# Top-k attention and a gated MLP on one core: the weight preparation spread over twelve slots for ten, and four steps of the opening moved

## The chip, the core and the metric

The kernel runs on one core of a Trainium2 chip. The metric is device time in microseconds (us); lower is better. Five engines work in it, each through its own queue in order: TensorE (PE: matmuls, and PEld, the loading of their weights), VectorE (DVE), ScalarE (ACT), GpSimd (POOL), and SyncE (SP), which issues the DMAs. An engine waits only at the head of its queue, so one late operand holds everything that is queued behind it.

## The reference

Attention over 8 batches, 8 heads, 576 rows and a head dimension of 64, in which each row keeps its 32 largest scores, and then an MLP with a gate. Everything is float32.

```python
scores = scale * np.matmul(q, k.transpose(0, 1, 3, 2))
kth = np.partition(scores, -top_k, axis=-1)[..., -top_k:-top_k + 1]
scores = np.where(scores >= kth, scores, -1e9)
attn = np.exp(scores - np.max(scores, axis=-1, keepdims=True))
attn = attn / (np.sum(attn, axis=-1, keepdims=True) + 1e-09)
x = np.matmul(attn, v)                # to (4608, 512): heads side by side
h = x @ w_in                          # 512 to 2048
out = (h / (1 + np.exp(-1.702 * h))) @ w_out
```

## The kernel before

**Slots.** The attention is cut into 144 slots, 18 for each batch. A slot is 128 rows of two heads (or the 64 last rows of four). For a slot n the steps are, by function:

- `scores`: PE makes the 128x576 scores of two heads in PSUM (`s_ps`); ACT copies them to SBUF (`sc`, line 238).
- `topk`: DVE finds the 32 largest of each row by fourteen passes, eight of MAX8 (line 247) and six of MATCH_REPLACE8 (line 250).
- `bounds`: POOL makes two small tiles, `cut` and `low`, from the 32nd and the first value (lines 266 and 267).
- `exponentials`: ACT makes the masked exponentials `pr` (lines 275 and 277) and their sums `den`.
- `divide`: DVE makes 1/`den` (lines 286 and 288, tiles `some` and `rden`). For n below SETTLED, POOL then writes `by`, a diagonal of the reciprocals, two of 128x128 (line 292), of which there is one buffer; later, ACT and POOL scale one head of `pr` each (lines 294 and 295).
- `turn_main`, `turn_ends`: PE turns `pr` (line 308 by a matmul with `by`, line 306 by a plain transpose), and ACT copies the result to `pt` (line 316).
- `values`: PE multiplies with v (line 338), ACT copies to `xT` (line 350).

When the four head pairs of a row block are done, `hidden` (PE, line 381, four groups for one row block), `tanh` (ACT, line 398), `gate` (DVE, line 414, or with `aside` POOL, lines 411 and 412, which needs a copy `h` by ACT, line 401) and `project` (PE, line 429) do the MLP for it. `gT` has four buffers, so at most four gated groups wait for `project`.

**Weights.** A float32 weight is not used as it was loaded: `round_piece` remakes each of 32 pieces of 128x512 in steps on three engines: "size" (ACT, line 144), "shift" (DVE, line 145), "low" (ACT, line 147), "sign" (ACT, line 146), and "finish" (POOL, lines 140 and 141, two operations). The text calls "finish" a weight step. The pieces of slot n are loaded in slot n-1 and their finishes run in slot n+1; `raws` has eight buffers for the loads. The first 16 pieces are `win`, the others `wout`.

**The order.** It is written out by hand. `opening` prepares the first two head pairs. Then `slot(n)` runs for n = 0 to 9 (SETTLED = 9): the "single slots", which interleave topk(n) with the exponentials, the turning and the values of n-1, the scores of n+2, and the weight pieces of `by_slot[n]`. From slot 10 on, `two_slots(n)` handles two slots at a time: a "pair". Single slots use the DVE gate; pairs use POOL's. `project` starts in slot 8 (PROJECTS = 7). Inside topk, the queues are filled at set places:

```python
if i == 2 and unfinished:
    unfinished.pop(0)()           # one weight step
if i == 5:
    if before: divide(n - 1)
    while unfinished: unfinished.pop(0)()
```

In a pair, all weight steps left over go into topk at one a place, ahead of the POOL work of `divide` and of `gate`, and ahead of `bounds` of the next slot. `stay_warm` adds matmuls whose results nobody uses.

Of the kernel before, what the change touches and what calls it, by code (L numbers as in the profile page):

```python
# [28 lines left out]
def kernel(  # L29
# [37 lines left out]
    CC = C // P  # L67
    FC = DFF // P
    G = 4
# [7 lines left out]


    PROJECTS = 7
    SETTLED = 9  # L80
    assert D == 64 and 2 * TAIL == P and C == NP * P and C == PIECE and B % 2 == 0
    assert TOPK == 32 and NP == 4 and NF == 4 and NG == 4 and CC == 4

# [74 lines left out]
    def stay_warm(count, of=ident[:]):  # L158

        none = ps_p.tile([P, C], F32, name="none", tag="po")  # L160
        for i in range(count):
            nc.tensor.matmul(none[:, 0:P], lhsT=of, rhs=of, start=True, stop=True)
# [58 lines left out]
    def scores(n):  # L221
        b, t, hps = slots[n]
        ps = [ps_s.tile([P, 2, 512], F32, name="s_ps") for _ in range(2)]
        if t < NF:
            parts = [(i, 0, slice(0, P), slice(t * P, (t + 1) * P)) for i in range(2)]
        else:
            parts = [(i, p, slice(p * TAIL, (p + 1) * TAIL), slice(FULL, S)) for i, p in ((0, 0), (1, 1), (0, 1), (1, 0))]
        for c in range(2):
            for i, p, rows, cols in parts:
                on = slice(i * D, (i + 1) * D)  # L230
                nc.tensor.matmul(  # L231
                    ps[i][rows, c, 0:HALF],
                    lhsT=qT[b, hps[p]][on, cols],
                    rhs=kT[b, hps[p]][on, FIRST[i] + c * HALF : FIRST[i] + (c + 1) * HALF],
                )
        sc = st[n]["sc"] = scp.tile([P, 2, S], F32, name="sc")
        for i in range(2):
            nc.scalar.copy(out=sc[:, i, :].rearrange("p (c k) -> p c k", c=2), in_=ps[i][:, :, 0:HALF])  # L238
# [30 lines left out]
    def exponentials(n):  # L269

        sc, cut, low = st[n]["sc"], st[n]["cut"], st[n]["low"]
        pr = st[n]["pr"] = prp.tile([P, 2 * S], F32, name="pr")
        den = st[n]["den"] = small.tile([P, 2], F32, name="den")
        for i in range(2):
            nc.scalar.activation(sc[:, i, :], sc[:, i, :], AF.Prelu, bias=cut[:, i : i + 1], alpha=HUGE)  # L275
        for i in range(2):
            nc.scalar.activation(  # L277
                pr[:, i * S : (i + 1) * S], sc[:, i, :], AF.Exp, bias=low[:, i : i + 1],
                accum_out=den[:, i : i + 1],
            )  # L280
# [37 lines left out]
    def turn_main(n):  # L318
        for i in range(2):
            turn(n, i * NF, MAIN[i], NF)  # L320

    def turn_ends(n):

        turn(n, 2 * NF, FULL, 1)
# [122 lines left out]
    READY = (((-9, -8), (-7, -6), (-4, -3), (-2, -1)), ((-7, -6), (-4, -3), (-3, -2), (-1, -2)))  # L447
    FETCH = (((-13, -12), (-11, -10), (-7, -7), (-5, -4)), ((-11, -10), (-9, -8), (-5, -5), (-2, -2)))
    VALUES = ((-8, -7, 0, 0), (-8, -7, 2, 2))
    by_slot = dict(enumerate([2, 2, 3, 3, 3, 3, 4, 4, 4, 4]))  # L450
    for n in by_slot:
        first = sum(map(len, list(by_slot.values())[:n]))
        by_slot[n] = list(range(first, first + by_slot[n]))
# [9 lines left out]
    for b in range(1, B):  # L463
        for hp in range(NP):
# [2 lines left out]
                at(b * PER + READY[b % 2][hp][i], prepare, name, b, hp)  # L467
            at(b * PER + VALUES[b % 2][hp], load_v, b, hp)
    unfinished = []

    early = []

    def opening():

        stay_warm(7, v_ends[0][:].rearrange("p j d -> p (j d)"))
        for hp in range(2):
            for name in "qk":
                load(name, 0, hp)
        for x in by_slot[0]:
            load_piece(x)  # L480
        for m in range(2):
            for name in "qk":
                prepare(name, 0, m)
            if m == 1:
                early.extend(round_piece(x) for x in by_slot[0])
                for piece in early:
                    piece["size"]()
            scores(m)
        for hp in range(2, NP):
            for name in "qk":  # L490
                load(name, 0, hp)
        load_v(0, 0)
        for x in by_slot[1]:
            load_piece(x)

    def slot(n):
        todo = later.pop(n, [])
        for fn, args in todo:
            if fn is not prepare:
                fn(*args)  # L500
        preparing = [args for fn, args in todo if fn is prepare]
        settled = n > PROJECTS
        aside = SETTLED < n < N
        before = 0 <= n - 1 < N
        if before:
            bounds(n - 1)
            exponentials(n - 1)
        some = [round_piece(x) for x in by_slot.get(n, [])] if n else early
        if n == 0:
            for piece in some:  # L510
                piece["low"]()
                piece["sign"]()
        else:
            for piece in some[:2]:
                piece["size"]()
        if not settled:
            for args in preparing:
                prepare(*args)
            scores(n + 2)
            stay_warm(4)  # L520
        if n > 0:
            for piece in some[2:]:
                piece["size"]()
        tanh(aside)
        for i, op in enumerate(topk(n) if n < N else [lambda: None] * 14):
            op()
            if i == 2 and unfinished:
                unfinished.pop(0)()
            if i == 5:
                if before:  # L530
                    divide(n - 1)
                while unfinished:
                    unfinished.pop(0)()
            if i == 8 and not aside:
                gate(aside)
        for piece in some:
            piece["shift"]()
            unfinished.append(piece["finish"])
        if n == 0:
            return  # L540
        if aside:
            gate(aside)
        if settled:
            for args in preparing[:1]:
                prepare(*args)
        for piece in some[:2]:
            piece["low"]()
        going = settled and len(to_project) > (2 if n < N else 0)
        if going:
            project(range(G - 1))  # L550
        if before:
            turn_main(n - 1)
        if going:
            project(range(G - 1, G))
        if before:
            turn_ends(n - 1)
        for piece in some[2:]:
            piece["low"]()
        if before:
            values(n - 1)  # L560
        for piece in some:
            piece["sign"]()
        if settled and n + 2 < N:
            scores(n + 2)
        if settled:
            for args in preparing[1:]:
                prepare(*args)
        if not ready and not settled:
            stay_warm(4)
        hidden()  # L570

    def two_slots(n):

        first, second = [later.pop(m, []) for m in (n, n + 1)]
        get = lambda todo: [args for fn, args in todo if fn is prepare]

        preparing = [get(first)[:1], get(second)[:1], get(first)[1:], get(second)[1:]]

        def begin(todo):
            for fn, args in todo:  # L580
                if fn is not prepare:
                    fn(*args)

        def prepare_some():
            for args in preparing.pop(0):
                prepare(*args)

        live = lambda m: 0 <= m < N
        going = lambda: len(to_project) > (2 if n < N else 0)
        aside = n < N  # L590

        def soften(m):
            if live(m):
                bounds(m)
                exponentials(m)

        def find(m):
            for i, op in enumerate(topk(m) if live(m) else [lambda: None] * 14):
                op()
                if i == 5 and live(m - 1):  # L600
                    divide(m - 1)
                if i > 1 and unfinished:
                    unfinished.pop(0)()

        def middle(m):
            go = going()
            if go:
                project(range(G - 1))
            if live(m) and "pr" in st[m]:
                turn_main(m)  # L610
            if go:
                project(range(G - 1, G))
            if live(m) and "pr" in st[m]:
                turn_ends(m)

        begin(first)
        soften(n - 1)
        tanh(aside)
        find(n)
        gate(aside)  # L620
        prepare_some()
        middle(n - 2)
        hidden()
        begin(second)
        soften(n)
        tanh(aside)
        gate(aside)
        prepare_some()
        middle(n - 1)
        find(n + 1)  # L630
        prepare_some()
        for m in (n + 2, n - 2, n - 1, n + 3):
            if m > n and live(m):
                scores(m)
            elif m < n and live(m) and "pt" in st[m]:
                values(m)
        prepare_some()
        hidden()
# [41 lines left out]
```

## Time and profile before

| | |
|---|---|
| median of 6 runs | 1630.87 us (1627.9 to 1632.59) |
| the profiled execution | 1627.79 us, its span 1626.0 us |
| PE busy | 1583.0 us, 97% of the span |
| DVE busy | 1480.1 us, 91% |
| ACT busy | 1154.8 us, 71% |
| POOL busy | 753.0 us, 46% |
| chain that ended last | 88% PE, 5% ACT, 3% DVE |

All times below are from the start of the span. The profiled execution took 1.8 us more than its span, and was 3.1 us under the median. A "busy" sum is the time with at least one instruction of an engine under way; the "idle" of a row is the time in which its engine waited ahead of it, with the instruction that ended the wait. PEclk is the TensorE clock that was granted, as a share of the full one. A float32 matmul shows as two records in the trace and a transpose as one, so "x32" of a row of line 381 is one group of 16 matmuls.

### The profile page before, as it was taken

What the parts mean: (1) busy time and instruction counts of PE and PEld (TensorE: products, weight loads), DVE (VectorE), ACT (ScalarE), POOL (GpSimd) and SP (SyncE); (2) the same over time, 40 slices, a digit from 0 to 9 for tenths busy, and PEclk for the clock granted to TensorE, in tenths of its full rate; (3) what the DMA queues carried; (4) which work ended last, traced back from release to release, by engine and by line L of the source; (5) the groups of instructions that cost most, each with busy time, mean ns of one, the idle gap of its engine ahead of it and who ended that gap; (6) DMA issues with size and microseconds to landing.
All of it is one profiled execution on the core that took longest, in us unless ns stands there. A gap on an engine that the chain in (4) does not pass through costs nothing.

```text
span 1626.0 us, 32137 instructions
## 1 busy us (share of the span) xinstructions
PE 1583.0 (97%) x12025; PEld 1182.7 (73%) x12025; DVE 1480.1 (91%) x3212; ACT 1154.8 (71%) x2449; POOL 753.0 (46%) x782
## 2 busy tenths in 40 slices
PE   7787999999999999999999999999999999999999
PEld 5665677777777777777777777777777777777776
DVE  6999999999999999999999998999999999999960
ACT  6896776777777777777777777677777777777761
POOL 3788334444444444444444444444444444444430
PEclk8998999999999999999999999999999999999999
DMA  7342001110001001110001100011000100000000
GB/s 223 123 140 62 22 22 30 29 44 16 22 15 44 22 23 29 29 37 22 22 15 30 28 24 10 27 30 44 15 22 15 44 22 23 22 8 7 8 8 14
DMA packets 100636, 56.61 MB, mean 35 GB/s; under 512 B 83584, under 2 KB 91776, under 8 KB 100480
## 3 DMA queue, kind: packets, MB, share of 16 engines
q1 hardware_dynamic: 100480, 54.55, 11.9%
q8 instruction: 95, 1.56, 0.4%
q14 instruction: 61, 0.50, 0.1%
HBM read 45.09 MB, written 9.44 MB: 34 GB/s over the span
## 4 chain that ended last, share of the span: by engine, by line
PE 88%; ACT 5%; DVE 3%; POOL 1%; issue 1%; SPq 1%; DMA 0%; POOLq 0%; ACTq 0%
PE ph L381 30%; PE po L429 29%; PE o L338 9%; PE s_ps L231 9%; PE tp L306 8%; DVE top L247 2%; PE tp L199 1%; DVE left L250 1%; ACT sc L238 1%; ACT pr L277 1%; PE tp L308 1%; ACT raw L146 1%; POOL wout L140 1%; ACT sc L275 0%; ACT wout L144 0%
## 5 line engine op out<-in xcount | busy, mean ns | idle before, releaser
L247 DVE MAX8 top<-left 128x8 f32<-128x576 f32 x864 | 609.8, 747 | 0.0
L429 PE MATMUL po<-wout,gT 128*128 128x512 f32 x1152 | 541.6, 594 | 0.0
L381 PEld LDWEIGHTS ph<-xT,win 128*128 128x128 f32 x4096 | 467.4, 192 | 42.4 <-issue 40.6
L381 PE MATMUL ph<-xT,win 128*128 128x128 f32 x4096 | 484.7, 277 | 0.6 <-ACT h L401 0.6
L250 DVE MATCH_REPLACE8 left<-top,left 128x576 f32<-128x576 f32 x576 | 423.4, 743 | 0.0
L295 POOL TENSOR_SCALAR pr<-pr,rden 128x576 f32<-128x576 f32 x135 | 233.1, 1726 | 355.7 <-ACT th L398 347.5
L411 POOL TENSOR_SCALAR th<-th 128x512 f32<-128x512 f32 x133 | 198.7, 1494 | 224.2 <-ACT th L398 224.2
L429 PEld LDWEIGHTS po<-wout,gT 128*128 128x128 f32 x1152 | 197.8, 191 | 142.3 <-issue 141.6
L275 ACT ACTIVATE sc<-sc,cut 128x576 f32<-128x576 f32 x288 | 208.2, 774 | 129.1 <-POOL cut L266 126.7
L316 ACT COPY pt<-tp 128x512 f32<-128x512 f32 (+1 forms) x432 | 192.7, 480 | 146.8 <-PE tp L306 141.8
L306 PEld LDWEIGHTS tp<-ident,pr 128*128 128x128 f32 x1215 | 145.6, 141 | 114.6 <-issue 66.6
L238 ACT COPY sc<-s_ps 128x576 f32<-128x576 f32 x288 | 169.8, 644 | 74.7 <-PE s_ps L231 74.3
L277 ACT ACTIVATE pr<-sc,low 128x576 f32<-128x576 f32 x288 | 219.1, 764 | 0.0
L247 DVE MAX8 top<-sc 128x8 f32<-128x576 f32 x288 | 202.1, 743 | 11.6 <-ACT sc L238 11.6
L250 DVE MATCH_REPLACE8 left<-top,sc 128x576 f32<-128x576 f32 x288 | 211.6, 742 | 0.0
L306 PE MATMUL tp<-ident,pr 128*128 128x128 f32 x1215 | 177.7, 273 | 9.7 <-ACT q_t L201 8.5
L231 PE MATMUL s_ps<-k_t,q_t 64*128 64x288 f32 (+1 forms) x1280 | 182.0, 431 | 1.0 <-ACT k_t L201 1.0
L412 POOL TENSOR_TENSOR gT<-th,h 128x512 f32<-128x512 f32 x133 | 169.7, 1276 | 11.1
L338 PE MATMUL o<-pt,v_l 128*64 128x128 f32 (+1 forms) x2560 | 157.3, 266 | 1.7 <-ACT pt L316 0.8
L338 PEld LDWEIGHTS o<-pt,v_l 128*64 128x64 f32 x2560 | 130.1, 137 | 31.4 <-ACT pt L316 16.2
L231 PEld LDWEIGHTS s_ps<-k_t,q_t 64*128 64x128 f32 (+1 forms) x1280 | 99.5, 177 | 59.9 <-issue 40.5
L266 POOL TENSOR_SCALAR cut<-top 128x2 f32<-128x2 f32 x144 | 38.0, 264 | 209.5 <-DVE top L247 207.8
(55 smaller groups left out, 1177.5 us busy)
## 6 DMA issues: line engine op xcount, KB each, us to landing
q_l<-in_q_dram SPq DMA_DIRECT2D x64, 128.0 KB, 2.9
k_l<-in_k_dram SPq DMA_DIRECT2D x64, 128.0 KB, 2.8
raw<-in_moe_w_in_dram SPq DMA_DIRECT2D x16, 512.0 KB, 4.8
v_l<-in_v_dram SPq DMA_DIRECT2D x32, 256.0 KB, 3.0
raw<-in_moe_w_out_dram SPq DMA_DIRECT2D x16, 512.0 KB, 3.3
out_dram<-ob SPq DMA_DIRECT2D x32, 256.0 KB, 2.3
ends<-in_q_dram SPq DMA_DIRECT2D x32, 32.0 KB, 2.4
ends<-in_k_dram SPq DMA_DIRECT2D x32, 32.0 KB, 2.5
```

The costliest lines, as they stand in the source:

```text
L231: nc.tensor.matmul(ps[i][rows, c, 0:HALF], lhsT=qT[b, hps[p]][on, cols], rhs=kT[b, hps[p]][on, FIRST[i] + c * HALF : FIRST[i] + (c + 1) * ...
L247: nc.vector.max(top[:, i, 8 * r : 8 * r + 8], (left if r else sc)[:, i, :])
L250: nc.vector.match_replace(left[:, i, :], top[:, i, 8 * r : 8 * r + 8], (left if r else sc)[:, i, :], LOWEST)
L275: nc.scalar.activation(sc[:, i, :], sc[:, i, :], AF.Prelu, bias=cut[:, i : i + 1], alpha=HUGE)
L277: nc.scalar.activation(pr[:, i * S : (i + 1) * S], sc[:, i, :], AF.Exp, bias=low[:, i : i + 1], accum_out=den[:, i : i + 1],)
L295: nc.gpsimd.tensor_scalar(pr[:, S : 2 * S], pr[:, S : 2 * S], rden[:, 1:2], None, op0=ALU.mult)
L306: nc.tensor.transpose(tp[:, c * P : (c + 1) * P], pr[:, at], ident[:])
L316: nc.scalar.copy(out=to, in_=tp[:, 0 : blocks * P])
L338: nc.tensor.matmul(o[j * D : (j + 1) * D, 0 : cols.stop - cols.start], lhsT=main[:, j, c, :] if c < NF else tail[:, j, :], rhs=pt[:, j * N ...
L381: nc.tensor.matmul(ph[:, i, :], lhsT=win[:, c, f * P : (f + 1) * P], rhs=xT[:, c, :], start=(c == 0), stop=(c == CC - 1),)
L411: nc.gpsimd.tensor_scalar(th[:], th[:], 1.0, None, op0=ALU.add)
L429: nc.tensor.matmul(po[:], lhsT=gT[:, i, :], rhs=wout[:, f, :], start=(f == 0), stop=(f == FC - 1))
```

## The change

SETTLED goes from 9 to 11, so there are twelve single slots, 0 to 11, and pairs from slot 12 on. The 32 weight pieces are dealt over these twelve slots. Four more things move:

- `copy_scores` is taken out of `scores`. In single slots the ACT copy of the scores of n+1 now comes right behind the exponentials of n-1, one slot after its matmuls (it stood behind the matmuls of n+2 before). In pairs it stays where it was.
- Slot 0 is turned and multiplied with v in slot 2, not in slot 1: its turn stands at the head of slot 2's PE queue, and its `values` behind the scores of slot 4.
- Two weight steps are issued ahead of each division in a single slot, where it was one.
- `project` also counts the finished pieces (`may_project`): it does not start a group whose weights are not issued yet. In a pair, a group that would be the fourth waiting is projected at once.

```diff
-    SETTLED = 9
+    SETTLED = 11
@@ scores
+        st[n]["ps"] = ps
+
+    def copy_scores(n):
+        ps = st[n].pop("ps")
         sc = st[n]["sc"] = scp.tile([P, 2, S], F32, name="sc")
@@
-    by_slot = dict(enumerate([2, 2, 3, 3, 3, 3, 4, 4, 4, 4]))
+    by_slot = dict(enumerate([2, 2, 2, 3, 3, 3, 3, 4, 3, 3, 2, 2]))
@@
+    def finish_one():
+        unfinished.pop(0)()
+        finished.append(None)
+
+    def may_project(waiting):
+        return len(to_project) > waiting and len(finished) >= NG * CC + (to_project[0][1] + 1) * G
@@ slot(n)
             exponentials(n - 1)
+            copy_scores(n + 1)
+        if n == 2:
+            turn_main(0)
+            turn_ends(0)
...
             scores(n + 2)
+            if n == 2:
+                values(0)
             stay_warm(4)
...
-            if i == 2 and unfinished:
-                unfinished.pop(0)()
+            if i == 2:
+                for _ in range(min(2, len(unfinished))):
+                    finish_one()
...
-        going = settled and len(to_project) > (2 if n < N else 0)
+        going = settled and may_project(2 if n < N else 0)
+        before = before and n > 1
...
             scores(n + 2)
+            if n == SETTLED:
+                copy_scores(n + 2)
@@ two_slots(n): middle
-            go = going()
+            if len(to_project) > 3:
+                project(range(G))
+            go = may_project(2 if n < N else 0)
@@ two_slots(n): scores of the next slots
                 scores(m)
+                copy_scores(m)
```

More of the change, by code (lines that the diff above doesn't have):

```diff
@@ L471 @@
     early = []
+    finished = []
+    def finish_one():
[3 more added lines that the diff above has]
+        return len(to_project) > waiting and len(finished) >= NG * CC + (to_project[0][1] + 1) * G
     def opening():
@@ L532, in slot @@
                 while unfinished:
-                    unfinished.pop(0)()
+                    finish_one()
             if i == 8 and not aside:
@@ L588, in two_slots @@
         live = lambda m: 0 <= m < N
-        going = lambda: len(to_project) > (2 if n < N else 0)
         aside = n < N
@@ L602, in find @@
                 if i > 1 and unfinished:
-                    unfinished.pop(0)()
+                    finish_one()
         def middle(m):
-            go = going()
+            if len(to_project) > 3:
+                project(range(G))
+            go = may_project(2 if n < N else 0)
             if go:
@@ L634, in two_slots @@
                 scores(m)
+                copy_scores(m)
             elif m < n and live(m) and "pt" in st[m]:
```

## The prediction

> **What bounds the kernel.** I read the page's busy slices first, then the busy time in stretches, then the timelines of the engines up to 190 us. In the slices, the span in 40 parts of 40.65 us, PE is full from the fifth on, DVE ahead of that:
>
> ```profile
> PE   7787999999999999999999999999999999999999
> DVE  6999999999999999999999998999999999999960
> ```
>
> The stretches (columns: length, then busy us and records of PE, PEld, DVE, ACT, POOL; granted clock, DMA share, GB/s) put numbers to it:
>
> ```profile
> 20.00:188.40 168.40, 135.47 (x1001) 105.67 (x1001) 156.93 (x331) 135.85 (x277) 118.75 (x120) 0.92 0.36 117
> 188.40:300.00 111.60, 110.97 (x920) 81.68 (x919) 104.68 (x230) 81.14 (x178) 50.27 (x52) 1.00 0.11 30
> 300.00:1560.00 1260.00, 1259.50 (x9664) 940.69 (x9662) 1194.48 (x2604) 908.05 (x1934) 575.62 (x592) 1.00 0.09 23
> ```
>
> From 188.4 us to the end of DVE's work PE lacks 1.1 us of 1371.6, while DVE is idle for 72 us. So from there the time is PE's own work, and what a change gains before then arrives at the end one for one. Before then DVE sets the pace (156.9 busy of 168.4), and PE stands for 33 us.
>
> 188.4 us is a mark, the end of the first MLP group after slots 12 and 13. The two programs' orders, compared engine by engine, have the same PE rows behind it, and ahead of it the same groups, scores, turns, values, 21 blocks of projection from slot 8's first turn on, and filler matmuls. So the forecast is: where is the mark after?
>
> ```profile
> 149.45 0.60 PE L306 MATMUL tp<-ident,pr 128*128 128x128 f32 x4
> 158.56 1.09 PE L306 MATMUL tp<-ident,pr 128*128 128x128 f32 x4 [8.50 <-ACT q_t L201]
> ...
> 184.73 3.84 PE L381 MATMUL ph<-xT,win 128*128 128x128 f32 x32
> 188.41 0.60 PE L199 MATMUL tp<-ident,q_l 128*128 128x128 f32 x4
> ```
>
> This is PE's timeline; its largest stop is in the first pair. The timelines of POOL and ACT show why: slot 9's four weight steps, one head of `pr` and a gate all stand on POOL ahead of slot 10's `cut`, whose values DVE had ready at 149.7, and ACT waits for it with PE's buffers behind:
>
> ```profile
> 152.52 1.26 POOL L412 TENSOR_TENSOR gT<-th,h 128x512 f32<-128x512 f32 x1
> 153.75 0.23 POOL L266 TENSOR_SCALAR cut<-top 128x2 f32<-128x2 f32 x1
> ```
>
> ```profile
> 154.01 1.44 ACT L275 ACTIVATE sc<-sc,cut 128x576 f32<-128x576 f32 x2 [8.90 <-POOL cut L266]
> ```
>
> DVE's own timeline shows its three losses: the division that waits for ACT, the shifts (three in 1.08 us, then four in 4.07), and a division that lasts 1.28 us for 0.14:
>
> ```profile
> 38.84 0.17 DVE L286 TENSOR_SCALAR some<-den 128x2 f32<-128x2 f32 x1 [2.13 <-ACT pr L277]
> 44.67 1.08 DVE L145 TENSOR_SCALAR win<-win 128x512 uint32<-128x512 uint32 x3
> 128.25 0.14 DVE L286 TENSOR_SCALAR some<-den 128x2 f32<-128x2 f32 x1
> 134.66 4.07 DVE L145 TENSOR_SCALAR wout<-wout 128x512 uint32<-128x512 uint32 x4
> 142.76 1.28 DVE L286 TENSOR_SCALAR some<-den 128x2 f32<-128x2 f32 x1
> 157.00 0.17 DVE L286 TENSOR_SCALAR some<-den 128x2 f32<-128x2 f32 x1 [3.12 <-ACT pr L277]
> ```
>
> The slots began, by the first MAX8 on `sc`, at 11.25, 21.57, 32.52, 45.66, 58.50, 70.43, 82.54, 95.02, 109.67, 124.15, 138.66, 149.70 and 164.27 (slot 12).
>
> **The change, part by part, in DVE's time up to slot 12.**
>
> *Slot 0 turned in slot 2.* In slot 1 ACT has no copies of a turn and values before the next exponentials, so slot 2's division loses its 2.1 us wait. But slot 2's ACT queue then holds two turns: 2.85 us exponentials, 1.1 score copy, 1.3 `pt`, 1.2 sizes, `xT` with its wait for PE to 8.5, 1.2 low, the second `pt` to 11.9, `xT` 13.3, 1.2 signs: 14.5 us in a slot of 10.7. Slot 3's division so waits some 2.6 us where it waited 0.78. Sum −0.3. POOL's `by` has one buffer; slot 1's must wait for slot 0's turn, about 6 us into slot 2, no later than its own place.
>
> *Shifts.* The 32 took 20.8 us (7.9 and 12.9); unhindered, at 0.33, they take 10.6. The excess falls in slots 3, 4, 7, 8 and 9 (1.05, 1.03, 1.97, 2.65, 2.7: 9.4), where POOL is still in a weight step at the slot's end. With three pieces and two steps ahead of the division, POOL fills the 2.0 us for which it waited for `rden`, and is done some 9 us into a slot whose shifts start at 10 to 11. Only slot 8 follows four pieces; I leave it 1.0 and take −8.4. The ends are −9.4 and, were every slot as slot 3 was, nothing.
>
> *Two steps ahead of the division.* This is the price. A step is 2.65 us (1.37 and 1.28 from start to start); the first starts 0.28 us into a slot, so the second's latter half runs from 4.28 to 5.6. The division comes at 4.10 to 4.13. It either gets in between the halves, for some 0.1 us, or waits for the second, as at 142.76, for up to 1.3. Eleven slots do this, 1 to 11. Where `den` is late (slot 3, perhaps 4) it surely falls into that half. I take 0.1 in seven and 0.7 in four, 3.5 us in all; the ends are 0.5 and 12. `by` also starts at 5.7 for 4.6, and PE and ACT behind it go 1.1 later in each slot, which ACT's low steps mostly cover.
>
> Here the Trainium skill has a rule that speaks against the change: by "SBUF — State Buffer", section "Who interferes with whom", a two-port VectorE operation such as a float32 tensor_scalar and a GpSimd operation exclude each other, and the later one waits for the whole of the other. The 1.28 us row agrees, but at 221.82 a `some` beside a 1.49 us `th` of POOL took 0.50 and ended 0.85 us before it. By the rule alone, each of the eleven divisions would be an even draw over the running half, 0.65 us each, 7 us for 3.5, and my forecast 3.5 us higher; I keep the value from the place in the rows.
>
> *Two more single slots.* Slots 10 and 11 lose the pair's waits: 3.12 for exponentials, 1.36 for scores at 164.27, and the 1.1 of the division at 142.76; −5.6. They gain two DVE gates at 0.69: +1.4. Their divisions use `by`: PE turns by a matmul (16 records in 1.9 to 2.05 us) and not by a transpose (8 in 0.88): 2 x 1.2 us more for PE.
>
> *Score copies.* Each is 1.1 us of ACT as before. PE's scores of n+2 now wait for the copies of n+1, at 5 us into a slot; PE stood there for `by` anyway (2.2 to 3.6 us), and the filler behind the scores then runs up to the turn. The scores are needed a full slot later. Taken at nothing. The ends: uncovered, 1.2 us of scores ahead of the turn in slots 2 to 7, +7; with the stops filled, −4.4, since three turns of before ran at a granted clock of 0.55 to 0.57 after such stops, 3.5 us for 2.05.
>
> *Loads.* SP issues the same 32, two to four a slot; 8 `raws` buffers hold 3+3 and two more, while 4+4+4 blocked SP (x12 took 42.2 us). Gates and ACT steps per piece are the same number. No gain, no loss.
>
> Sum: −0.3 −8.4 +3.5 −5.6 +1.4 = −9.4: slot 12 begins at 154.9.
>
> **From there to the mark.** PE's work from slot 8's first turn: 9.2 for the rest of slot 8 (129.42 to 138.60 in slot 9), 11.9 each for slots 9 and 10 (with 2.7 of projection), 8.8 for slot 11, which does not project, 0.7 to prepare, 11 projection blocks at 0.86, 1.9 for the turn, 7.2 for scores, values, scores, group: 61 us. Before, 73.5 us went by (114.95 to 188.4) for 58.6. Slot 8 begins at 109.7 −0.3 −4.05 (shifts) −0.7 (22 pieces done for 24) +2.6 (divisions) = 107.2, its turn at +6.3; with 2 us of small stops the mark is at 176.5 if PE never waits for DVE. If it does: slot 11 begins 11.8 ahead of slot 12 (10.1 for passes and division, 0.7 gate, 0.7 shifts, 0.3), at 143.1, its turn 6.1 later, 8.3 to its group's end, then 0.7 + 9.5 + 0.6 (the copy of `po` out) + 1.9 + 7.2: 177.4; with the stops of that path, up to 3, some 179. I take 179: a gain of 9.4 us. Against the profiled execution, 1627.8 − 9.4 = 1618.4; against the median, 3.1 higher, 1621.5.
>
> **The rivals.**
> 1. Every division waits for POOL in full: 11 x 1.1 = 12 for 3.5, a gain of about 1 to 2, 1629. For it, the 1.28 row; against it, 0.15 us of timing. Chance 0.13.
> 2. Few stops and no late ACT: slot 3's 2.6, the 3.5 and the 2 to 3 of stops fall away: a gain of 13 to 18, 1615. Chance 0.20.
> 3. Slower: ACT becomes the bound of the single slots. Its steps for three pieces sum to 11.5 us in a slot of 12, but slots 7 to 9 took 14.5 each, two of them with ACT waiting on POOL and PE; `by` is later and a copy now stands ahead of the sizes. If slots 3 to 11 all go at 14.5, slot 12 begins at 173, and the end is 9 us later: 1640. It decides from 13.5 us a slot on, 2 us of waits on ACT in each. Against it: PE's stops before the turns get filled. Chance 0.10.
> 4. DVE, not PE, is the bound after an earlier mark, and the gain is given back: 1631. DVE's 72 us idle speaks against it. Chance 0.05.
>
> My forecast has 0.52 (a gain of 4 to 13). A median of this kernel can tell about 0.2%, 3.3 us, from no change. Faster by more: 0.52 + 0.20 + a third of rival 1 = 0.76; the rest of rival 1 and rival 4 make 0.13 within; 0.11 slower. The range: a gain of 17.4 (rival 2) to one of 0.9 (the dear end of the divisions), 1613.5 to 1630.
>
> **What would show it.** Right: slot 12 near 155; PE's mark near 179 and full after it; no stop of 8 us around the first pair; shifts near 0.33 us each but in slot 8; `some` mostly under 0.3 us. Wrong: `some` at 1.2 us in most slots (rival 1); slots 4 to 11 at 13.5 us with divisions waiting on `pr` (rival 3); PE idle behind the mark (rival 4). A mark that moves and an end that does not move by as much would overturn the whole reading.

## The result, and the profile after

Measured: 1626.78 us after (18 runs) against 1630.39 before (36 runs), a ratio of 0.9976 with a 95% interval of 0.9969 to 0.9982: 3.9 us gained, 2.9 to 5.1 by the interval. The forecast was a gain of 9.4. The direction held; the size was off by more than half. That the time lies in the range is luck: the range's slow end was worked out for blocked divisions, and it was the score copies that cost the time.

The two profiled executions differ by less, 1627.49 us (span 1625.7) against 1627.79, since the one of before lay 2.6 us under its median and the one of after 0.7 over its own. Their traces are read for where the time is, not for the 3.9.

The page's busy slices after, beside those of before:

```profile
PE   8788999999999999999999999999999999999999
DVE  7789999999999999999999998999999999999960
```

PE is fuller in the first and the fourth slice; DVE is fuller in the first and emptier in the second and third. The busy time in the same stretches as before (same columns: length, PE, PEld, DVE, ACT, POOL, clock, DMA, GB/s):

```profile
20.00:188.40 168.40, 144.12 (x1025) 112.27 (x1026) 152.01 (x334) 135.39 (x275) 113.61 (x118) 0.92 0.36 118
188.40:300.00 111.60, 111.16 (x922) 81.87 (x921) 104.69 (x230) 80.91 (x177) 50.65 (x52) 1.00 0.11 30
```

PE shows 8.7 us more busy before the mark for nearly the same work (24 records more), and DVE 4.9 less. PE's timeline at the mark:

```profile
184.63 3.84 PE L385 MATMUL ph<-xT,win 128*128 128x128 f32 x32
188.30 0.60 PE L199 MATMUL tp<-ident,q_l 128*128 128x128 f32 x4
```

The mark is at 188.30; it was at 188.41, and 179 was forecast. Where the time went shows in the starts of the slots on DVE: 11.01, 21.33, 31.91, 42.48, 56.01, 69.66, 85.04, 98.75, 115.00, 127.90, 140.41, 151.59, 164.32.

| slots | before | after | forecast after |
|---|---|---|---|
| 0 to 2 | 34.4 us | 31.5 | 32 |
| 3 to 7 | 64.0 | 72.5 | some 63 |
| 8 to 11 | 54.6 | 49.3 | 48 |

Slots 3 to 7 gave back 8.5 us, all that the rest had gained in this execution. DVE's timeline shows what lengthens them, the division of slots 3 to 5 for example (the idle time stands in brackets):

```profile
48.72 0.63 DVE L290 TENSOR_SCALAR some<-den 128x2 f32<-128x2 f32 x1 [2.06 <-ACT pr L281]
62.83 0.17 DVE L290 TENSOR_SCALAR some<-den 128x2 f32<-128x2 f32 x1 [2.64 <-ACT pr L281]
76.75 0.17 DVE L290 TENSOR_SCALAR some<-den 128x2 f32<-128x2 f32 x1 [2.91 <-ACT pr L281]
```

From slot 3 to slot 7 each division waits 1.2 to 2.9 us for exponentials. The waits of all engines between 42 and 116 us (columns: who waited for whom, us in total, times, longest) name what holds ACT:

```profile
PE s_ps L231 <- ACT sc L242: 13.2, 5, 4.4
ACT pt L320 <- PE tp L312: 11.8, 10, 2.7
DVE some L290 <- ACT pr L281: 11.7, 5, 2.9
```

PE and ACT wait for each other in a ring, and DVE waits for ACT. Slot 4 shows one turn of it, first on ACT, then on POOL, then on PE:

```profile
62.71 1.15 ACT L242 COPY sc<-s_ps 128x576 f32<-128x576 f32 x2
...
68.97 0.59 ACT L320 COPY pt<-tp 128x512 f32<-128x512 f32 x1 [2.29 <-PE tp L312]
```

```profile
63.37 1.19 POOL L296 TENSOR_SCALAR by<-ident,rden 128x128 f32<-128x128 f32 x2 [0.48 <-DVE rden L292]
```

```profile
63.37 2.82 PE L231 MATMUL s_ps<-k_t,q_t 64*128 64x288 f32 x8 [4.36 <-ACT sc L242]
66.12 1.92 PE L162 MATMUL none<-ident 128*128 128x128 f32 x8
67.88 1.95 PE L312 MATMUL tp<-by,pr 128*128 128x128 f32 x16
```

PE's next scores need the PSUM tiles that ACT empties behind its exponentials, so PE stands for 4.4 us. `by` is begun as PE's scores begin and is done at 64.6, but the turn is behind the scores in the queue and behind the filler, and both run slowly (the granted clock was 0.50 in 63.4 to 66.1 us): 2.82 us for 1.24, 1.92 for 1.16. The turn starts at 67.88; ACT has run out of other work and waits 2.3 us for it; its next exponentials are late by that; so are the next division and the next copies. In slot 4 of the kernel before, scores and filler were over when the wait began, and the turn followed `by` at once:

```profile
57.82 1.24 PE L231 MATMUL s_ps<-k_t,q_t 64*128 64x288 f32 x8
58.99 1.16 PE L162 MATMUL none<-ident 128*128 128x128 f32 x8
63.78 3.53 PE L308 MATMUL tp<-by,pr 128*128 128x128 f32 x16 [3.63 <-POOL by L292]
```

### The profile page after: what moved, and what is told of

Its sections match the earlier page's. It is cut to its first block, busy times and chain, and to the rows that moved or that the text cites. A ratio compares the mean times of both kernels' runs of the same rounds, so it can differ in the third digit from the quotient of the medians.

```text
span 1625.7 us, 32166 instructions
## 1 busy us (share of the span) xinstructions
PE 1591.9 (98%) x12047; PEld 1189.9 (73%) x12047; DVE 1475.2 (91%) x3214; ACT 1154.4 (71%) x2445; POOL 749.1 (46%) x780
## 4 chain that ended last, share of the span: by engine, by line
PE 89%; ACT 5%; DVE 4%; issue 1%; POOL 0%; DMA 0%; SPq 0%; POOLq 0%; ACTq 0%
PE ph L385 30%; PE po L433 29%; PE s_ps L231 10%; PE o L342 10%; PE tp L310 8%; DVE top L251 2%; DVE left L254 2%; PE tp L199 2%; ACT sc L242 1%; ACT pr L281 1%; ACT raw L146 1%; PE tp L312 1%; PE none L162 1%; ACT sc L279 0%; ACT pt L320 0%
## 5 line engine op out<-in xcount | busy, mean ns | idle before, releaser
L231 PE MATMUL s_ps<-k_t,q_t 64*128 64x288 f32 (+1 forms) x1280 | 189.0, 438 | 14.3 <-ACT sc L242 13.2
L310 PE MATMUL tp<-ident,pr 128*128 128x128 f32 x1197 | 174.2, 273 | 0.3 <-ACT k_t L201 0.3
L231 PEld LDWEIGHTS s_ps<-k_t,q_t 64*128 64x128 f32 (+1 forms) x1280 | 103.5, 180 | 74.4 <-issue 40.4
```

The costliest lines, as they stand in the source:

```text
L231: nc.tensor.matmul(ps[i][rows, c, 0:HALF], lhsT=qT[b, hps[p]][on, cols], rhs=kT[b, hps[p]][on, FIRST[i] + c * HALF : FIRST[i] + (c + 1) * ...
L310: nc.tensor.transpose(tp[:, c * P : (c + 1) * P], pr[:, at], ident[:])
```

## The experiments

Theory A: this ring is the loss, and it is one of queue order: the score copies now stand behind the exponentials while PE's scores stand ahead of the turn. Rival B: the second weight step makes `by`, and so the turn, late. Rival C: the two turns in slot 2 put ACT behind, and it carries that to slot 8. All ratios are to the kernel before, run on the same chip; a thousandth is 1.63 us.

**e1: the copies behind their matmuls again.**

```diff
             exponentials(n - 1)
-            copy_scores(n + 1)
...
             scores(n + 2)
+            copy_scores(n + 2)
```

> The changed kernel, but in single slots the score copies stand behind their matmuls again, as before the change. Theory A (in slots 3 to 7 PE's scores of n+2, which stand ahead of the turn of n-1, now wait for a copy behind the exponentials; PE comes to them cold, and ACT, DVE wait for the late turn in a ring): slots 3 to 7 fall from 72.5 us in all to about 63, the mark comes at 179 to 181, the median at 1618 to 1620. Rival B (the two weight steps make `by` and so the turn late): no change, 1626 to 1628. Rival C (the two turns in slot 2 put ACT behind, and it never catches up until slot 8): slot 3 still waits 2 us, gain under 3, 1624 to 1627.

1618.08 us, 0.9923 (0.9909 to 0.9936). Repeated, for a trace:

> The changed kernel with the score copies behind their matmuls again, a second time, for its trace. Theory A: 1617 to 1620; slots 3 to 7 take about 63 us in all, the mark comes at 179 to 181, PE's scores in slots 3 to 7 start without a wait for ACT.

1617.00 us, 0.9918 (0.9905 to 0.9932). The copies cost the change 8.6 to 9.5 us of a gain that was 12.6 to 13.4 without them. The mark is at 179.82, and slots 3 to 7 take 63.4 us. In PE's timeline at the same place, slot 4, the scores run early and the turn waits for `by` alone:

```profile
57.92 1.24 PE L231 MATMUL s_ps<-k_t,q_t 64*128 64x288 f32 x8
59.09 1.16 PE L162 MATMUL none<-ident 128*128 128x128 f32 x8
64.27 3.52 PE L312 MATMUL tp<-by,pr 128*128 128x128 f32 x16 [4.02 <-POOL by L296]
```

**e4: the copies stay where the change put them; PE's order is mended.** In slots 2 to 7 the scores go behind the values, as they do from slot 8 on.

```diff
-            scores(n + 2)
             if n == 2:
                 values(0)
+            if n < 2:
+                scores(n + 2)
             stay_warm(4)
...
-        if settled and n + 2 < N:
+        if n > 1 and n + 2 < N:
             scores(n + 2)
```

> The changed kernel, but in slots 2 to 7 PE's scores of n+2 stand behind the values of n-1, as they do from slot 8 on; the filler stays ahead of the turn. Theory A: nothing that waits for ACT stands ahead of the turn any more; slots 3 to 7 fall to 61 to 63 us in all, the mark to 177 to 180: 1616 to 1620. Rival B: the turn waits for `by` as late as before: 1625 to 1627. Rival C: 1625 to 1627.

1617.12 us, 0.9920 (0.9907 to 0.9934); mark at 176.11, slots 3 to 7 in 61.1 us. That is no better than e1, where neither the copies nor the scores are moved: together the two moves gain nothing over leaving both. Its waits between 42 and 103 us have no row for scores; what is left of the division's is short:

```profile
PE tp L312 <- POOL by L296: 11.1, 5, 3.2
DVE some L290 <- ACT pr L281: 1.6, 2, 1.0
```

So it is not ACT's order by itself, nor `by`, nor what slot 2 leaves behind: those are the same in e4 as in the change. It is the scores' place ahead of the turn.

**e7: the copies alone, on the kernel before.**

> The kernel before with the score copies alone moved behind the exponentials in single slots, and nothing else of the change. Theory A: the ring alone, 7 to 10 us slower than the kernel before: 1637 to 1641. If the copies only hurt together with the two steps ahead of the division (which make `by` late), no change: 1629 to 1632.

1642.19 us, 1.0068 (1.0054 to 1.0082): 11 us slower, a little over the upper end. The loss does not need the two steps. Slot 2 of its trace takes 17.2 us (31.89 to 49.04), where it had taken 13.1.

**e6: the filler ahead of the turn left out in slots 2 to 7.**

> The changed kernel without the four filler matmuls that stand between the scores and the turn in slots 2 to 7 (they compute nothing that is used). Theory A: the filler is part of the ring, 1.2 us on a full clock and 1.9 to 2.1 on the half clock that PE has after its wait; without it the turn comes that much earlier in slots 3 to 7, 5 to 8 us in all, less what a colder PE costs: 1619 to 1624. If the filler pays for itself by warming the clock, 1626 to 1630.

1620.50 us, 0.9941 (0.9927 to 0.9954): 5.7 us better than the change. The filler was part of the ring, and did not pay for itself there.

**e2: one weight step ahead of the division.**

> The changed kernel, but with one weight step ahead of each division, as before the change. Theory A: slots 3 to 7 keep their length, since the turn there waits for the scores and not for `by`; slots 8 to 10 get their slow shifts back at 1 to 2 us a slot: 1627 to 1631. Rival B: `by` comes 1.1 us earlier in each of slots 3 to 7, and they shorten by 5 us or more in all: 1620 to 1622. Rival C: no change in slots 3 to 7.

1631.97 us, 1.0009 (1.0001 to 1.0018): the second step is worth 5.4 us in the change, a little over theory A's range. In its trace slots 3 to 7 keep their length (72.1 us for 72.5). This is the end of rival B.

**e3: slot 0 turned in slot 1.**

> The changed kernel, but slot 0 is turned and multiplied in slot 1, as before the change. Theory A: the ring sets the length of slots 3 to 7 whatever came before; slot 2 gets a wait back and slot 3 loses one, within 2 us of the changed kernel, 1625 to 1629. Rival B: the same. Rival C: ACT starts slot 3 some 2 us earlier and slots 3 to 7 are 12 to 12.5 us each: 1618 to 1622.

1632.38 us, 1.0011 (1.0002 to 1.0020). Rival C had the sign wrong, but theory A missed as well: 5.7 us worse where at most 2 was expected. In its trace the ring has taken slot 2 too, 17.4 us. Whether that is all was tried without the ring:

**e10: the spreading and the two steps alone** (the copies and slot 0 as before the change).

> The kernel before with twelve single slots and two weight steps ahead of each division alone: the copies and slot 0 stay as before the change. Theory A: turning slot 0 in slot 2 mattered only because the ring would take slot 2 as well (it took 17 us there where slot 0 stayed in slot 1); without the ring it is worth 0 to 2 us: 1617 to 1620. If it has its own worth of 5 us: 1622 to 1624.

1623.47 us, 0.9951 (0.9937 to 0.9966). Against e1, the same kernel with slot 0 turned late, that is 4.6 to 5.4 us, so slot 0's place has its own worth, and this part of theory A fell. DVE's timeline in its slot 2, and POOL's, show it:

```profile
42.16 0.64 DVE L290 TENSOR_SCALAR some<-den 128x2 f32<-128x2 f32 x1 [4.71 <-ACT pr L281]
```

```profile
33.54 1.28 POOL L140 TENSOR_TENSOR win<-win,raw 128x512 int32<-128x512 int32 x1
38.87 1.29 POOL L141 TENSOR_TENSOR win<-win,raw 128x512 f32<-128x512 f32 x1 [4.04 <-ACT raw L146]
```

ACT's end of slot 1, with the turn of slot 0 in it, now runs on into slot 2: POOL waits 4.0 us for a sign step and the division 4.7 for its exponentials, where these were 1.46 and 2.13 before. The turn in slot 1 comes late, but not for `by`. First POOL and PE in e10, then PE before:

```profile
27.25 1.19 POOL L296 TENSOR_SCALAR by<-ident,rden 128x128 f32<-128x128 f32 x2 [0.33 <-DVE rden L292]
32.98 2.85 PE L312 MATMUL tp<-by,pr 128*128 128x128 f32 x16
```

```profile
30.55 1.95 PE L308 MATMUL tp<-by,pr 128*128 128x128 f32 x16
```

In e10 `by` is done at 28.4, and PE comes to the turn 4.5 us later, behind scores and filler on a granted clock of 0.50 (28.5 to 34.0 us); before, the clock was 1.00 there (28.1 to 32.5). The second weight step is not needed for this: in e9 (below), whose slots 0 and 1 are those of the kernel before, the turn starts at 31.65 and the division of slot 2 waits 3.71. Why the clock differs so between executions stays open.

**e5: ten single slots, with the other three parts changed.**

> The changed kernel, but with ten single slots and the weight pieces dealt as before the change; the copies, slot 0 and the two steps stay changed. Theory A with its prices so far (two steps worth 5 us, slot 0 worth 5, the copies costing 9): the shifts of slots 8 and 9 and the first pair are slow again, and what the spreading gains is the rest, 2 to 4 us: 1629 to 1632. A rival that puts the whole gain down to the spreading: 1634 or more.

1633.54 us, 1.0026 (1.0016 to 1.0036): between the two expectations. The spreading is worth 8.2 us within the change, more than the 2 to 4 that I had left for it. In its trace the shifts are hardly slower than in the change (13.1 us for 12.8), and slots 3 to 7 take 73.8 us for 72.5. Most of the loss is in slots 8 and 9, with four pieces each: 30.3 us for 25.4.

**e8: the scores last, and the copies right behind them.**

> The changed kernel with PE's scores behind the values in slots 2 to 7 and with the score copies right behind their matmuls too. Theory A: once nothing stands between the copy and the turn, the place of the copy on ACT hardly matters, within 3 us of the two kernels that had one of the two: 1615 to 1620. If the later copies are a gain in themselves once PE's order is mended (ACT does not wait for PE's scores before it goes on): 1619 to 1623.

1621.27 us, 0.9938 (0.9924 to 0.9952): 2.9 us over e4. Once PE's order is mended, the later copy tends to be the better of the two places, though the two intervals overlap.

**e9: the scores last, on the kernel before.**

> The kernel before with PE's scores behind the values in slots 2 to 7, and nothing of the change. Theory A: in the kernel before, the scores waited for nothing and held up no turn, so the order of PE alone gains nothing: 1629 to 1633. If PE's order were worth something by itself: under 1627.

1633.41 us, 1.0015 (1.0006 to 1.0024). The mended order gains nothing alone; it costs 2.4 us there, and pays only where the copies are late.

## Why the prediction was wrong

**The mark: right.** From the mark to the end of the span the traces agree within 0.7 us: 1437.6 us before, 1437.4 after, 1436.9 in e1's second run, 1437.4 in e4 and e6, 1437.6 in e9. What the opening gains arrives at the end, and rival 4 is out.

**The score copies: the step that failed.** They were "taken at nothing", with the reason that "PE stood there for `by` anyway". It did stand there, but at a place in the queue behind the scores; after the change it stands ahead of them, and then has scores and filler to do before the turn, on a slow clock. There was nothing left to cover them, since both waits hang on the same exponentials: the copy follows these on ACT, `by` follows them through DVE and POOL. The step had the scores start "at 5 us into a slot"; in slots 3 to 7 they started 6.0 to 7.6 us into it, in slot 4 with `by` itself (63.37). The end of +7 that the step gave as "uncovered" was the right case and too small: 8.6 to 9.5 us within the change, 11 alone. It priced only 1.2 us of scores; on a mean granted clock of 0.50 to 0.63 they took 2.7 to 2.8 in slots 3 to 6, and the filler 1.8 to 2.1. And it took PE's wait as an end, without following who waits for PE: ACT for the turn, DVE for ACT, and then PE's own next scores.

**Slot 0 in slot 2: mis-sized.** The sum had −0.3; e10 against e1 measures about −5. Slot 2 went as worked out (10.6 us for 10.7), and slot 3's division waited 2.1 us and then 0.5 more (2.6 forecast). What was wrong is the other side: the cost of leaving slot 0 in slot 1 was read from one execution of the kernel before, 2.1 us; the same wait is 4.7 in e10 and 3.7 in e9, where PE's clock was at 0.50 ahead of slot 1's turn.

**Two steps ahead of the division: right in size.** The sum had −8.4 for shifts, by the steps and the three pieces a slot together, and +3.5 for blocked divisions. In the traces the 32 shifts went from 20.8 us to 12.8 (6.9 and 5.9), and in slots 1 to 11 the divisions took 2.1 us in all beyond 0.15 each (the row below also has slot 12's, of 1.22):

```profile
L145 DVE TENSOR_SCALAR wout<-wout 128x512 uint32<-128x512 uint32 x16 | 6.9, 481 | 0.0
L145 DVE TENSOR_SCALAR win<-win 128x512 uint32<-128x512 uint32 x16 | 5.9, 413 | 0.0
L290 DVE TENSOR_SCALAR some<-den 128x2 f32<-128x2 f32 x12 | 4.9, 412 | 12.9 <-ACT pr L281 12.9
```

The idle column of the last row is mostly the ring: 12.9 us, for 6.3 before. The divisions fell on both sides of the gap, as forecast: 0.15 us in slots 1, 2, 8 and 10, and 0.63, 1.16 and 0.66 in slots 3, 9 and 11; in slots 4 to 7 they came late and took 0.17. Without the ring the same excess is 1.8 us in e1's second run and 4.5 in e10. The value from the rows' places, 3.5, was nearer to the 2.1 measured than the estimate of 7 by a rule that the later operation always waits in full (the Trainium skill, "SBUF — State Buffer", section "Who interferes with whom"). The second step alone is worth 5.4 us (e2). In e2's trace the shifts take 15.6 us, so 5.2 of the 8.0 us that they lost were lost without it; `some` (the same eleven slots) takes 1.8. These two rows do not add up to 5.4; slot 11's division waits 3.9 us there, for 1.0 in the change.

**Two more single slots: right in kind.** Slots 10 and 11 took 11.2 and 12.7 us for 11.0 and 14.6, and PE's 8.5 us stop is gone. They gained 1.7 us where the sum had 4.2: four shifts (1.5 us) moved into them, and slot 11's division still waited 1.0.

**Rival 3** came near it, at a smaller scale: five slots at 13.5 to 16.3 us, not nine at 14.5, with divisions that wait for `pr`. It had ACT held by POOL and PE; in these slots it was PE alone. Its argument against, "PE's stops before the turns get filled", was the mistake: they were filled with work that stood ahead of the turn. Without the copies the forecast was 9.4 and the measurement 12.6 to 13.4; the difference, 3.2 to 4.0, is somewhat less than slot 0's 5.

## What to carry to other kernels

When a copy out of PSUM is moved later, go to the instruction that needs the PSUM tile again and list what stands behind it in its queue; an engine's idle time covers moved work only if that work can start well before the idle time ends. Here the scores and the operand that PE idled for were released by the same exponentials. A wait that returns to its own engine (PE for ACT, ACT for PE) is priced once around the ring, with the clock that PE has after the wait. Filler matmuls are not free where something ahead of them in the queue comes late: here they stood behind scores that waited, and leaving them out gained 5.7 us. A wait that is read from one execution is a weak price: slot 0's place was worth 0.3 us by the one trace, and about 5 between two kernels that differ in nothing else.

## What the runs showed of the hardware

The length of the last wait did not tell the speed of the matmuls behind it. In slot 5 of the change PE waited 1.72 us, to 77.30, and since 63.37 no other wait in its rows was over 0.31 us. The granted clock was 1.00 from 71.0 to 78.0 us and 0.50 from 78.0 to 81.0, so it fell 0.7 us after the scores had begun; they took 2.71 us, where 1.24 is usual. In e1's second run a turn after a wait of 2.67 us took 2.05, on a clock of 1.00. The Trainium skill, "TensorE: Matmul & The Clock Gate", section "What's actually happening", gives about 3.4 us of idle for the drop to half the clock. The first of these rows differs from that: there 1.72 us, half of that, came before the drop. What the clock goes by, these rows do not show.
